# Cached attention decode: V of six head groups loaded through ScalarE's DMA queue beside K on SyncE's queue

## Chip, cores and metric

One core of a Trainium2 chip. The metric is the device time of one execution in microseconds (us). The kernel before takes 203.48 us, median of 3 runs (203.31 to 203.59). The span of a profile is about 1.3 us shorter than the time of the same run.

## The reference

One token goes through a layer norm, a query projection, attention over 4096 cached keys and values in each of 32 heads, an output projection, and a gated MLP. K and V are 33.5 MB each; all weights together are 17 MB, so 84 MB are read for very little arithmetic.

```
q = x_ln @ wq                                # 640 -> 32 heads x 128
scores = einsum("bhqd,bhkd->bhqk", q, k_cache) * 128**-0.5
o = einsum("bhqk,bhkd->bhqd", softmax(scores), v_cache)
h = x + o @ wo
h2 = h + (gelu(h_ln @ w_gate) * (h_ln @ w_up)) @ w_down
```

## The kernel before

The heads are taken in 8 groups of 4. K of a group is one transfer of 4 MB, V another (32 KB of contiguous bytes in each of 128 partitions). The sixteen transfers go in a fixed order through three buffers: transfer n lands in buffer n mod 3 and may be issued when transfer n-3 has been consumed. All are issued by SyncE, so they form one queue.

```
order = [("K", 0), ("V", 0), ("K", 1)]
for G in range(1, NG - 1):
    order += [("K", G + 1), ("V", G)]
order.append(("V", NG - 1))
# K0 V0 K1 K2 V1 K3 V2 K4 V3 K5 V4 K6 V5 K7 V6 V7

def issue(upto):
    while state["next"] < min(upto, len(order)):
        n = state["next"]
        kind, g = order[n]
        # (cut: source, destination)
        landed[n] = [P.dma("sync", dst[...], src[...],
                           consumed[n - NSLOT] if n >= NSLOT else None) for i in range(parts)]
        state["next"] = n + 1
```

K is consumed by four VectorE multiplies (`score_mult`); a chain of identity matmuls on PE (`fold`) and a VectorE reduction sum the products; ScalarE's exponentials of each of the four follow (`score_exp`, which also holds the reduction). V is consumed by 32 matmuls (`pv_group`). PE does them in the order of the list, so V of group G-1 is consumed just after the scores of group G.

```
def scores(G):
    for i in range(4):
        score_mult(4 * G + i)                  # waits for K; the 4th one frees K's buffer
        if i >= 1:
            score_exp(4 * G + i - 1)
    score_exp(4 * G + 3)
    issue(pos[("K", G)] + 1 + NSLOT)           # into K(G)'s buffer: V(G), for G >= 2

for kind, G in order:
    if kind == "K":
        scores(G)
        continue
    # (cut: sums and head sums)
    heads = pv_group(G)                        # frees V's buffer
    issue(pos[("V", G)] + 1 + NSLOT)           # into V(G)'s buffer: K(G+3), for G >= 1
```

After the last V come the loads of the output projection and, into the freed buffers, of the MLP weights.

The softmax here doesn't subtract the row's maximum and nothing guards it: scores larger than these inputs give would overflow.

## Time and profile before

| | before |
|---|---|
| time, median | 203.48 us |
| bytes read | 84.3 MB |
| DMA queue q1 (SyncE), share of 16 engines | 97.8% |
| PE / VectorE / ScalarE busy | 60% / 50% / 30% |
| VectorE waiting for K | 32.9 us, 7 times |

These are lines of the profile's page. The rows `DMA` and `GB/s` cut the span in 40 equal slices: a 9 means that the 16 DMA engines were busy 90% or more of the slice. Below them are the DMA queues with packets, bytes and share of engine time, and the page's list of issues, with median us from issue to landing.

```profile
DMA  9999999999999999999999999999999999999992
GB/s 357 414 417 454 428 415 422 428 451 441 423 422 428 428 444 441 428 417 428 422 448 448 418 422 430 422 441 448 428 425 422 409 428 445 409 405 439 406 412 111
...
q1 hardware_dynamic: 4322, 84.32, 97.8%
...
q10 hardware_dynamic: 2, 0.00, 0.0%
...
slot<-in_A_k_cache_dram SPq DMA_DIRECT2D x8, 4096.0 KB, 21.6
slot<-in_A_v_cache_dram SPq DMA_DIRECT2D x7, 4096.0 KB, 17.7
```

The DMA engines are never without work until the last slice. In the trace's packet records (start, duration, size and queue of every packet, read from the packed trace; no view of the page prints them), successive K and V transfers start 9.7 us apart, a 32 KB packet takes 1.213 us, and 16 engines at that rate move 432 GB/s. 84.3 MB at that rate is 195 us: the kernel runs at its floor but for its start and tail.

Packet times in this text count from the same zero as the profile's timelines. The prediction and the expectations below were written with packet times counted from a zero about 0.35 us later, so their 1.4 or 1.3 us from an issue to its first packet is 1.0 us here, and their 3.8 to 4.5 us is 3.4 to 4.1 us.

The next view gives the busy time of each engine in five stretches: start and end, length, then the engines in the order of its first line (PEld is PE's weight load), the clock granted to PE, the DMA share and GB/s.

```profile
core 0: us, PE busy (x) PEld busy (x) DVE busy (x) ACT busy (x) POOL busy (x), PEclk, DMA share, GB/s
65.00:80.00 15.00, 9.90 (x72) 4.61 (x71) 10.36 (x9) 6.14 (x29) 0.00 (x0) 1.00 0.99 425
80.00:110.00 30.00, 19.17 (x121) 8.43 (x123) 17.49 (x15) 13.10 (x63) 0.00 (x0) 0.83 1.01 433
110.00:120.00 10.00, 5.75 (x35) 2.24 (x25) 5.54 (x4) 0.91 (x3) 0.00 (x0) 0.83 0.99 424
120.00:150.00 30.00, 20.11 (x140) 8.57 (x138) 17.93 (x15) 13.97 (x66) 0.00 (x0) 0.89 1.01 434
150.00:160.00 10.00, 5.55 (x14) 1.97 (x15) 6.41 (x4) 1.17 (x6) 0.00 (x0) 0.66 0.96 415
```

Three lines of VectorE's timeline (start, duration, then the instruction) and one of the table of waits (total us, times, longest) show the rhythm around 58 and 74 us:

```profile
57.65 4.48 DVE L261 TENSOR_TENSOR prod<-slot,qb 128x4096 bf16<-128x4096 bf16 x2
...
66.04 2.28 DVE L261 TENSOR_TENSOR prod<-slot,qb 128x4096 bf16<-128x4096 bf16 x1
...
74.26 4.50 DVE L261 TENSOR_TENSOR prod<-slot,qb 128x4096 bf16<-128x4096 bf16 x2 [3.25 <-DMA slot<-in_A_k_cache_dram]
```
```profile
DVE prod L261 <- DMA slot<-in_A_k_cache_dram: 32.9, 7, 6.7
```

VectorE starts K of group 2 at 57.65 us without waiting, frees its buffer with the fourth multiply at 68.32, and then waits a few us for each later K. While VectorE waits for K, K is on its way, and the DMA engines are busy.

### The profile page before, as it was taken

The page shows a single profiled execution, that of the slowest core. Times are in us where ns is not written, and L with a number is a line of the kernel's source. Part 1 is how long each engine was busy: PE and PEld are TensorE (multiplying, and loading weights), DVE is VectorE, ACT ScalarE, POOL GpSimd, SP SyncE. Part 2 cuts the span into 40 slices and gives each one's busy share as a digit, 9 for nine tenths or more (in the row PEclk, how much of TensorE's full clock was granted, in tenths as well). Part 3 has the DMA queues.
Part 4 walks back from the last instruction along what each step waited for, and adds up shares of the span by engine and source line. Part 5 has one row for each costly group of instructions (what it writes and reads, how often), then busy time and mean ns, then how long its engine had stood idle before and what let it go on. Part 6 is the DMA issues. An engine that isn't in the chain of part 4 may idle for free.

```text
span 202.0 us, 2498 instructions
## 1 busy us (share of the span) xinstructions
PE 121.3 (60%) x1009; PEld 58.5 (29%) x1009; DVE 100.7 (50%) x104; ACT 61.1 (30%) x273; POOL 4.1 (2%) x12
## 2 busy tenths in 40 slices
PE   0108067367749847660978196628744987467395
PEld 0103022112213322230324032312331334267383
DVE  3101179428979739814792677277718760100221
ACT  2011005610563642550156125503640364100101
POOL 7000000000000000000000000000000000000000
PEclk9999859966996999995599979966996699955555
DMA  9999999999999999999999999999999999999992
GB/s 357 414 417 454 428 415 422 428 451 441 423 422 428 428 444 441 428 417 428 422 448 448 418 422 430 422 441 448 428 425 422 409 428 445 409 405 439 406 412 111
DMA packets 4335, 84.47 MB, mean 418 GB/s; under 512 B 482, under 2 KB 868, under 8 KB 1508
## 3 DMA queue, kind: packets, MB, share of 16 engines
q1 hardware_dynamic: 4322, 84.32, 97.8%
q8 instruction: 8, 0.13, 0.3%
q14 instruction: 3, 0.02, 0.0%
q10 hardware_dynamic: 2, 0.00, 0.0%
HBM read 84.31 MB, written 0.00 MB: 417 GB/s over the span
## 4 chain that ended last, share of the span: by engine, by line
DMA 64%; PE 17%; DVE 14%; issue 2%; SPq 2%
DMA slot<-in_A_k_cache_dram 42%; DVE prod L261 12%; PE bank L269 11%; DMA slot<-in_B_w_down_dram 11%; DMA slot<-in_A_v_cache_dram 11%; PE bank L298 3%; SPq L51 2%; DVE sc L276 1%; PE bank L307 1%; PE bank L434 0%; DVE out_row L443 0%; PE bank L318 0%; DVE RT L317 0%
## 5 line engine op out<-in xcount | busy, mean ns | idle before, releaser
L269 PE MATMUL bank<-prod,id_b 128*128 128x512 bf16 x256 | 74.1, 448 | 50.5 <-DVE prod L261 50.5
L261 DVE TENSOR_TENSOR prod<-slot,qb 128x4096 bf16<-128x4096 bf16 x32 | 72.4, 2285 | 32.9 <-DMA slot<-in_A_k_cache_dram 32.9
L280 ACT ACTIVATE p_bd<-sc,zero_t 32x32 bf16<-32x32 f32 x128 | 46.4, 362 | 84.7 <-DVE sc L276 83.5
L269 PEld LDWEIGHTS bank<-prod,id_b 128*128 128x128 bf16 x256 | 26.5, 111 | 98.9 <-DVE prod L261 64.4
L276 DVE TENSOR_REDUCE sc<-bank 128x32 f32<-128x512 f32 x32 | 22.0, 688 | 19.6 <-PE bank L269 19.5
L280 ACT ACTIVATION_READ_ACCUMULATOR p_bd<-sc,zero_t 32x1 f32 x128 | 23.5, 184 | 0.0
L298 PE MATMUL bank<-slot,p_bd 128*16 128x512 bf16 x256 | 18.8, 409 | 3.1 <-ACT p_bd L280 2.5
L298 PEld LDWEIGHTS bank<-slot,p_bd 128*16 128x16 bf16 x256 | 9.7, 93 | 8.3 <-ACT p_bd L280 3.0
L307 PE MATMUL bank<-po_sb,hs 128*16 128x128 f32 x64 | 8.4, 274 | 1.1 <-ACT po_sb L302 1.1
L336 PE MATMUL bank<-aP,arena 128*128 128x1 bf16 x160 | 6.7, 178 | 3.8 <-DMA arena<-in_A_wo_dram 3.8
L404 PE MATMUL bank<-hlnT,slot 128*128 128x1 bf16 (+1 forms) x140 | 6.7, 176 | 3.2 <-DMA slot<-in_B_w_gate_dram 3.2
L302 ACT COPY po_sb<-bank 128x512 f32<-128x512 f32 x8 | 4.7, 585 | 11.1 <-PE bank L298 11.1
L247 PE MATMUL bank<-arena,xlnB 128*32 128x512 bf16 x40 | 4.5, 629 | 5.5 <-DMA arena<-in_A_wq_dram 5.5
L336 PEld LDWEIGHTS bank<-aP,arena 128*128 128x128 bf16 x160 | 6.6, 131 | 3.9 <-DMA arena<-in_A_wo_dram 2.6
L404 PEld LDWEIGHTS bank<-hlnT,slot 128*128 128x128 bf16 (+1 forms) x140 | 6.3, 118 | 4.1 <-issue 3.8
L232 ACT ACTIVATE ln<-ln,eps_t 128x1 f32<-128x1 f32 x2 | 0.6, 294 | 21.6 <-DVE ln L230 21.6
L307 PEld LDWEIGHTS bank<-po_sb,hs 128*16 128x16 f32 x64 | 5.5, 96 | 4.4 <-issue 2.1
L221 PE MATMUL bank<-one_bf,x_row 1*128 1x1 bf16 x5 | 0.4, 177 | 8.2 <-DMA x_row<-in_A_x_dram 8.2
L391 DVE TENSOR_TENSOR hT<-xx,bank 128x5 f32<-128x5 f32 x1 | 0.2, 161 | 10.2 <-PE bank L336 10.2
L251 DVE CAST qb<-bank 128x512 bf16<-128x512 f32 x1 | 0.7, 692 | 8.4 <-PE bank L247 8.4
L247 PEld LDWEIGHTS bank<-arena,xlnB 128*32 128x32 bf16 x40 | 1.6, 139 | 7.6 <-issue 7.6
L322 DVE TENSOR_SCALAR aT<-bank,rz 16x128 bf16<-16x128 f32 x2 | 0.7, 338 | 6.0 <-PE bank L307 6.0
(59 smaller groups left out, 24.7 us busy)
## 6 DMA issues: line engine op xcount, KB each, us to landing
slot<-in_A_k_cache_dram SPq DMA_DIRECT2D x8, 4096.0 KB, 21.6
slot<-in_A_v_cache_dram SPq DMA_DIRECT2D x7, 4096.0 KB, 17.7
arena<-in_A_wq_dram SPq DMA_DIRECT2D x1, 5120.0 KB, 15.0
slot<-in_A_v_cache_dram SPq DMA_DIRECT2D x2, 2048.0 KB, 19.9
arena<-in_A_wo_dram SPq DMA_DIRECT2D x1, 2560.0 KB, 27.5
slot<-in_B_w_gate_dram SPq DMA_DIRECT2D x1, 2160.0 KB, 15.4
arena<-in_A_wo_dram SPq DMA_DIRECT2D x1, 1920.0 KB, 31.6
slot<-in_B_w_up_dram SPq DMA_DIRECT2D x1, 1296.0 KB, 18.1
```

The source lines that it names most:

```text
L51: ev = self.op(eng, lambda e: e.dma_start(out, in_), *deps, dma=True)
L247: i = e.matmul(ps_q[hf][32 * j:32 * j + 32, :], xlnB[:, c, :], wq_j[:, c, j, 4 * hf:4 * hf + 4, :], start=(c == 0), stop=(c == 4))
L251: qa = V(lambda e: e.tensor_copy(qb[:, 0:4, :].rearrange("p g d -> p (g d)"), ps_q[0][:, :]), qd)
L261: m = V(lambda e: e.tensor_tensor(out=prod[:, s % 4, :, :], in0=kt[:, 32 * u:32 * u + 32, :], in1=qb[:, G, :].unsqueeze(1).to_broadcast([1 ...
L269: i = e.matmul(ps_f[s % 2][:, :], id_b[:, :], prod[:, s % 4, :, 16 * b:16 * b + 16], start=(b == 0), stop=(b == 7))
L276: reds[s] = V(lambda e: e.reduce_sum(sc[:, s % 4, :], ps_f[s % 2][:, :].rearrange("p (g d) -> p g d", d=16), axis=AX.X), folds[s], exps.ge ...
L280: x = A(lambda e, j=j: e.activation(p_bd[32 * j:32 * j + 32, G % 2, 32 * (s % 4):32 * (s % 4) + 32, j], sc[32 * j:32 * j + 32, s % 4, :], ...
L298: i = e.matmul(po[a:a + 16, :], p_bd[:, G % 2, 4 * b:4 * b + 4, :].rearrange("p g j -> p (g j)"), vt[:, 4 * b:4 * b + 4, :], start=(b < 4) ...
L302: evs[G] = A(lambda e: e.copy(po_sb[:, G % 2, :], po[:, :]), pvs[G], hds.get(G - 2))
L307: i = e.matmul(ps_a[0:16, 128 * (G // 4):128 * (G // 4) + 128], hs[:, r, 12 - 4 * g:28 - 4 * g], po_sb[:, G % 2, 128 * r:128 * r + 128], s ...
L336: r = e.matmul(ps_p[:, c:c + 1], wo_sb[:, t, i, c::5], aP[:, t, i:i + 1], start=(t == 0 and c == 0 and i == 0), stop=(t == 1 and i == 15), ...
L404: i = e.matmul(ps[0 if m < 13 else 64:128, m:m + 1], ws, hlnT[:, c:c + 1], start=(c == 0 and m == 0), stop=(c == 4), skip_group_check=True)
```

## The change

The intent is to let V travel beside K instead of behind it. V of groups 1 to 6 is issued by ScalarE. The second hunk moves the call of `issue` ahead of the last two groups of exponentials, since ScalarE, which now issues V(G), would otherwise reach the issue only after them. With every load on SyncE that hunk alone would change nothing, because it does not alter the order of any engine's own list (read from the code; not run).

```diff
             w = 128 * DH // parts
-            landed[n] = [P.dma("sync", dst[...], src[...], consumed[n - NSLOT] if n >= NSLOT else None)
+            queue = "scalar" if kind == "V" and 0 < g < NG - 1 else "sync"
+            landed[n] = [P.dma(queue, dst[...], src[...], consumed[n - NSLOT] if n >= NSLOT else None)
                          for i in range(parts)]
@@ def scores(G):
             score_mult(4 * G + i)
+            if i == 3:
+                issue(pos[("K", G)] + 1 + NSLOT)
             if i >= 1:
                 score_exp(4 * G + i - 1)
         score_exp(4 * G + 3)
-        issue(pos[("K", G)] + 1 + NSLOT)
```

(`[...]` marks cut index expressions.)

More of the change, by code (lines that the diff above doesn't have):

```diff
@@ L187, in issue @@
             w = 128 * DH // parts
-            landed[n] = [P.dma("sync", dst[:, i * w:(i + 1) * w], src[:, i * w:(i + 1) * w], consumed[n - NSLOT] if n >= NSLOT else None)
+            queue = "scalar" if kind == "V" and 0 < g < NG - 1 else "sync"
+            landed[n] = [P.dma(queue, dst[:, i * w:(i + 1) * w], src[:, i * w:(i + 1) * w], consumed[n - NSLOT] if n >= NSLOT else None)
                          for i in range(parts)]
```

## The prediction

> **What bounds it now.** The DMA engines. The slice view shows DMA at 9 tenths in 39 of 40 slices; the queue table gives SyncE's queue (q1) 97.8% of the 16 engines' span, 84.3 MB at a mean 417 GB/s. In the trace's packet records the fifteen 4 MB K/V transfers that are not split follow each other every 9.7 us without a gap, and a 32 KB packet takes 1.213 us (27 GB/s an engine, 432 GB/s for 16). All 84.3 MB at that rate is 195 us, so with about 1.4 us of start and 2.5 us of tail some 199 us of the 202 us span is a floor, whichever queue issues. The chain of waits agrees: 64% DMA. VectorE is at 50%; the waits view has it waiting 32.9 us for K (7 times).
>
> **What changes.** No byte, packet or arithmetic instruction is added or removed. Six V loads (25 MB) move to ScalarE's queue. An issue costs 0.33 us on the issuing sequencer (timeline), so ScalarE, idle 84.7 us before its exponentials, pays about 2 us in all, none of it critical. The issue, moved ahead of the last exponentials, waits for the group's last multiply, as they do anyway. SyncE gains nothing by not being held up: transfer n waits for the consumption of n-3, and consumption happens in issue order.
>
> What does change is order. The Trainium skill ("DMA: Bandwidth & Descriptors", section "Issuing engines are not separate DMA queues") says DMAs from both engines run on the same 16 DMA engines and interleave; "Queues, rings and completion order" says round-robin by packet. This trace agrees in one place: the 1.3 KB x load on ScalarE's queue took 1.57 us beside 40 KB packets of 1.51 us. So V(G) will no longer queue behind K(G+1) but halve its rate.
>
> **On the critical path.** My estimate, by replaying the traced durations (9.7 us a transfer alone, 10.1 to 11.8 us from K's landing to the last multiply, 4.7 to 5.7 us from there to the next K issue, 1.4 us from issue to first packet), with equal sharing: K of group 2 lands about 7 us later (54 to 61), VectorE starts it about 4 us later, K of group 4 starts about 4 us later (98), the others 1 to 4 us. But the engines have other work queued then, so lateness costs only where all three buffers are landed and unconsumed. That happens once, near 72 us, for about 1 us; elsewhere the backlog stays positive though thinner. V of the last group then lands about 1 us later (171.6 in the chain), and the 27 us of weights after it follow unchanged.
>
> **Prediction.** 204.5 us, range 202.8 to 208.5. Faster by over 2%: 0.02. Within 2%: 0.76. Slower by over 2%: 0.22.
>
> **What would show it.** Queue table: q1 about 70%, ScalarE's queue (q10) about 29%, sum near 97.5%, same MB. DMA issues: V about 20 us or more to landing (17.7 before), K near 20. A DMA slice below 9 only near 70 to 77 us. VectorE's wait for K up, with alternating long and short waits; ScalarE's busy time the same. The final weights stage as long as before.
>
> **What would make it wrong.** Unequal sharing: if V gets more than half, K is later, and idle DMA time grows to several us per early group. Two streams being slower per byte than one (32 KB packets over 1.22 us at equal load). Slower folds under a 0.5 clock, which empty the thin backlog in several cycles. A faster result would need engines above 27 GB/s, or an idle gap that I overlooked.

## The result

| | before | after |
|---|---|---|
| time, median | 203.53 us (6 runs, 203.31 to 205.04) | 209.28 us (6 runs, 208.87 to 211.11) |
| ratio, 95% interval | | 1.029 (1.024 to 1.034) |
| span of the profile | 202.0 us | 208.1 us |
| bytes read | 84.3 MB | 84.3 MB |
| ScalarE busy | 61.1 us | 61.1 us |

A ratio is the mean time of one kernel's runs over that of the other's runs of the same rounds, so it is not quite the ratio of the medians. The change is slower by 2.9%, above the range of the prediction.

The same lines of the page after. Slices are 5.2 us here; DMA falls below 9 in slices 14 and 15 (67.6 to 78.0 us) and 30 (150.9 to 156.1 us).

```profile
DMA  9999999999999789999999999999979999999992
GB/s 355 394 455 403 447 447 416 409 476 422 405 453 447 321 302 413 460 430 409 447 453 384 384 414 441 441 416 441 428 280 403 409 409 430 426 413 432 409 410 101
...
q1 hardware_dynamic: 3458, 59.15, 66.7%
q10 hardware_dynamic: 866, 25.17, 29.0%
...
slot<-in_A_k_cache_dram SPq DMA_DIRECT2D x8, 4096.0 KB, 23.8
slot<-in_A_v_cache_dram ACTq DMA_DIRECT2D x6, 4096.0 KB, 21.0
slot<-in_A_v_cache_dram SPq DMA_DIRECT2D x1, 4096.0 KB, 33.6
```

The two queues together are at 95.7% of a longer span. The five stretches after:

```profile
65.00:80.00 15.00, 12.55 (x79) 5.43 (x76) 12.28 (x9) 7.15 (x33) 0.00 (x0) 0.93 0.88 359
80.00:110.00 30.00, 15.88 (x80) 5.77 (x80) 14.46 (x12) 8.78 (x41) 0.00 (x0) 0.77 0.99 426
110.00:120.00 10.00, 8.09 (x66) 4.05 (x66) 8.31 (x9) 5.50 (x25) 0.00 (x0) 1.00 0.98 396
120.00:150.00 30.00, 14.35 (x89) 5.66 (x88) 13.81 (x13) 7.83 (x37) 0.00 (x0) 0.77 1.00 433
150.00:160.00 10.00, 7.87 (x63) 3.80 (x62) 8.61 (x7) 6.46 (x31) 0.00 (x0) 1.00 0.84 329
```

The reader should see that the engines move 426 to 433 GB/s where they have work, with two queues as with one, and that the loss sits in three short stretches: 359, 396 and 329 GB/s. To put a number on it, I add the bytes of the packet records in a stretch, divide by 433 GB/s, and call the rest of the stretch lost. This gives 2.6 us lost in 70 to 80 us, 1.0 in 110 to 120 and 2.5 in 150 to 160, against 0.1 in each before. That is about 5.9 us more than before (from unrounded figures), of the 208.1 - 202.0 = 6.1 us by which the spans differ. So nearly the whole loss lies in three places. About 4.0 us of it is time in which engines have no packet (1.9, 0.4 and 1.7 us); most of the rest is slow packets behind each gap: the sixteen that restart the engines at 74 us took 1.7 to 2.1 us each in place of 1.21.

VectorE's timeline shows what precedes the first of them, and ScalarE's and SyncE's queues show the issues (`ACTq`, `SPq`):

```profile
61.64 4.49 DVE L262 TENSOR_TENSOR prod<-slot,qb 128x4096 bf16<-128x4096 bf16 x2 [2.84 <-DMA slot<-in_A_k_cache_dram]
...
70.86 2.28 DVE L262 TENSOR_TENSOR prod<-slot,qb 128x4096 bf16<-128x4096 bf16 x1
...
75.75 4.49 DVE L262 TENSOR_TENSOR prod<-slot,qb 128x4096 bf16<-128x4096 bf16 x2
```
```profile
73.17 0.33 ACTq L51 DMA_DIRECT2D slot<-in_A_v_cache_dram  x1
```
```profile
77.86 0.33 SPq L51 DMA_DIRECT2D slot<-in_A_k_cache_dram  x1
```
```profile
DVE prod L262 <- DMA slot<-in_A_k_cache_dram: 37.8, 5, 12.7
```

K of group 2 is started at 61.64 us, 4.0 us later than before, since it shared the engines with V of group 1 (issued at 43.28). Its last multiply starts at 70.86 and frees the buffer at 73.14; V of group 2 is issued at 73.17. But the packet records show that the data of K of group 3 had all been moved by 73.62 on the slowest engine, and earlier on the others, while V of group 2 has its first packet at 74.15. V of group 1 had also landed (68.02) and was still waiting for its matmuls (75.59). In that moment one buffer is being consumed, two hold landed data, and nothing is left to transfer. The pattern repeats: the last multiplies of groups 4 and 6 come late in the same way, and their V issues (112.87 and 154.30 us) are followed by their first packets 1.0 us later.

### The profile page after: what moved, and what is told of

Its sections match the earlier page's. It is cut to its first block, busy times and chain, and to the rows that moved or that the text cites. A ratio compares the mean times of both kernels' runs of the same rounds, so it can differ in the third digit from the quotient of the medians.

```text
span 208.1 us, 2498 instructions
## 1 busy us (share of the span) xinstructions
PE 116.9 (56%) x1009; PEld 56.2 (27%) x1009; DVE 100.3 (48%) x104; ACT 61.1 (29%) x273; POOL 4.1 (2%) x12
## 3 DMA queue, kind: packets, MB, share of 16 engines
q10 hardware_dynamic: 866, 25.17, 29.0%
## 4 chain that ended last, share of the span: by engine, by line
DMA 66%; PE 14%; DVE 14%; issue 2%; SPq 2%
DMA slot<-in_A_k_cache_dram 46%; DVE prod L262 12%; DMA slot<-in_B_w_down_dram 11%; PE bank L270 10%; DMA slot<-in_A_v_cache_dram 9%; PE bank L299 3%; DVE sc L277 2%; SPq L51 2%; PE bank L308 1%; PE bank L436 0%; DVE out_row L445 0%; PE bank L319 0%; DVE RT L318 0%
## 5 line engine op out<-in xcount | busy, mean ns | idle before, releaser
L270 PE MATMUL bank<-prod,id_b 128*128 128x512 bf16 x256 | 69.9, 426 | 54.4 <-DVE prod L262 54.4
L262 DVE TENSOR_TENSOR prod<-slot,qb 128x4096 bf16<-128x4096 bf16 x32 | 72.4, 2282 | 37.8 <-DMA slot<-in_A_k_cache_dram 37.8
L270 PEld LDWEIGHTS bank<-prod,id_b 128*128 128x128 bf16 x256 | 25.2, 107 | 99.4 <-DVE prod L262 68.0
L299 PE MATMUL bank<-slot,p_bd 128*16 128x512 bf16 x256 | 18.1, 406 | 8.6 <-DMA slot<-in_A_v_cache_dram 6.1
L299 PEld LDWEIGHTS bank<-slot,p_bd 128*16 128x16 bf16 x256 | 8.3, 93 | 15.3 <-DMA slot<-in_A_v_cache_dram 7.3
## 6 DMA issues: line engine op xcount, KB each, us to landing
slot<-in_A_k_cache_dram SPq DMA_DIRECT2D x8, 4096.0 KB, 23.8
```

What stands on the lines that cost most here:

```text
L262: m = V(lambda e: e.tensor_tensor(out=prod[:, s % 4, :, :], in0=kt[:, 32 * u:32 * u + 32, :], in1=qb[:, G, :].unsqueeze(1).to_broadcast([1 ...
L270: i = e.matmul(ps_f[s % 2][:, :], id_b[:, :], prod[:, s % 4, :, 16 * b:16 * b + 16], start=(b == 0), stop=(b == 7))
L299: i = e.matmul(po[a:a + 16, :], p_bd[:, G % 2, 4 * b:4 * b + 4, :].rearrange("p g j -> p (g j)"), vt[:, 4 * b:4 * b + 4, :], start=(b < 4) ...
```

## Experiments

**Theory A.** The loss is one of order. V takes half of the engines from the K that is needed next, K lands late, its buffer comes free late, and by then the other two buffers have landed, so the DMA engines idle. **Rival B.** Issuing from ScalarE costs in itself, by its waits or its late issues. **Rival C.** Two busy queues carry fewer bytes per us than one. All times below are medians, ratios are against the kernel before in the same rounds, and "lost" is the DMA time lost between 44 and 172 us, worked out as above (before 0.7, after 6.5 us). All twelve kernels gave correct results.

### Dose: which V loads go to ScalarE's queue

```diff
-            queue = "scalar" if kind == "V" and 0 < g < NG - 1 else "sync"
+            queue = "scalar" if kind == "V" and g in (1, 3, 5) else "sync"     # odd
+            queue = "scalar" if kind == "V" and g in (2, 4, 6) else "sync"     # even
+            queue = "scalar" if kind == "V" and g == 1 else "sync"             # first
```

(One of the three lines at a time.)

> Only V of groups 1, 3 and 5 on ScalarE's queue, the other three on SyncE's. Theory A: each of these is issued while the next K has most of its 4 MB to go, so K of groups 2, 4, 6 stays late and the three idle gaps stay: 207 to 209.5 us, nearly the whole loss. Rival B or C (a cost per V load on ScalarE's queue, or per byte that two queues carry): half the loss, about 206.4 us.

> Only V of groups 2, 4 and 6 on ScalarE's queue. Theory A: in the order of before these are issued when the K ahead of them has half or less to go, and a queue that joins waits about 3.8 us before its first packet, so they share almost nothing: 203.5 to 204.5 us, no gap. Rival B or C: half the loss, about 206.4 us.

> Only V of group 1 on ScalarE's queue. Theory A: K of group 2 lands at 60 to 61 us in place of 54, one idle gap of about 2 us near 73 us, none later: 205 to 206.5 us. Rival B or C: one sixth of the loss, about 204.5 us.

| | time | ratio (95%) | lost |
|---|---|---|---|
| odd | 211.10 us | 1.039 (1.036 to 1.042) | 7.7 us |
| even | 204.28 us | 1.006 (1.003 to 1.008) | 1.5 us |
| first | 205.56 us | 1.010 (1.009 to 1.012) | 2.6 us |

The stretches of the run with V of group 1 alone on ScalarE's queue:

```profile
65.00:80.00 15.00, 13.34 (x79) 5.69 (x77) 12.12 (x10) 7.15 (x33) 0.00 (x0) 0.87 0.90 366
80.00:110.00 30.00, 17.93 (x96) 7.29 (x93) 18.02 (x15) 12.12 (x58) 0.00 (x0) 0.83 1.01 434
110.00:120.00 10.00, 5.50 (x49) 2.98 (x50) 4.68 (x4) 2.16 (x9) 0.00 (x0) 0.83 0.99 424
```

One moved V load makes one gap (366 GB/s in the first stretch), 30 us after its issue, and none later. Equal numbers of moved loads cost 7.7 us and about 0.9 us, depending on which they are. That refutes a cost per load (B) and a cost per byte on a second queue (C) as the main cause: both expected half the loss in either run. By the packet records the K ahead still has about half of its 4 MB to go (47 to 53%) when an odd V has its first packet; for the even ones it is 5, 25 and 43%. So "share almost nothing" holds for V of group 2 alone: K of groups 5 and 7 were started at 118.08 and 157.99 us in place of 113.12 and 152.10. The first of these delays is followed by the only loss worth naming, 0.8 us near 130 us, so "no gap" was not fully met; the second costs nothing, as the last V and the projection weights had been issued by 150.1 us and kept the engines supplied. In these runs how late a K is does not tell the cost; what else is queued then does. The run "odd" lies above my range of 207 to 209.5 us: its gaps are where they were expected, lost 2.0, 2.0 and 3.4 us, but the third is larger than with all six loads moved. Why, I did not settle.

### One queue, issued by ScalarE

```diff
-            queue = "scalar" if kind == "V" and 0 < g < NG - 1 else "sync"
+            queue = "scalar" if n >= NSLOT else "sync"        # and all weights on "scalar"
```

> Every load from the fourth K/V transfer on, and the weights, issued by ScalarE on its one queue, in the order of the kernel before; SyncE keeps only the first four loads and the output. Theory A (loss comes from K and V sharing the engines through two queues): no sharing, so 203.5 us within 1%, no DMA slice under 9. Rival B (issuing V from ScalarE costs in itself, by the issue or by waits in ScalarE's program): at least as slow as the change, 209 us or more.

Measured: 212.93 us, ratio 1.047 (1.046 to 1.048). This fits rival B at first sight, but the trace shows two faults of the experiment. The fourth transfer, K of group 2, joined on ScalarE's queue while K of group 1 was still moving on SyncE's; K of group 1 was started at 49.36 us in place of 44.18, and a gap of 3.5 us followed in 70 to 80 us. And the output-projection loads stood behind ScalarE's own work and were issued 27 us late, so the engines were nearly empty again from about 174 to 178 us. From 80 to 172 us, on one queue, nothing was lost. I built it again without the handover and with the projection loads issued right behind the last V:

```diff
-    d_x = P.dma("scalar", x_row[:, :], A_x[0, :, :])
-    d_wq = [P.dma("sync", arena[:, :], ...)]
+    d_wq = [P.dma("scalar", arena[:, :], ...)]     # x now on "sync"
@@ issue()
+            queue = "scalar"                        # every load; also wo, w_gate, w_up, w_down
# (cut: the load of ScalarE's activation table, now behind the first K issue)
@@ main loop, after issue() behind pv_group(G)
+        if G == NG - 3:
+            wo_load(...)                            # three calls, moved up from below the loop
```

> Mends the first one-queue test, which shared the engines for one transfer at the handover and issued the output-projection weights 27 us late, both by its own build. Now every load but x, from the first on, is on ScalarE's queue in the order of before, the projection weights right behind the last V. Theory A: 203.5 to 205.5 us (up to 2 us for a later first issue and for ScalarE's own work ahead of the last weights), no DMA gap between 40 and 170 us. Rival B (issuing from ScalarE costs): 209 us or more, or gaps in the middle.

Measured: 203.41 us, ratio 1.000 (0.998 to 1.002). Rival B is refuted: ScalarE can issue every large load and the time is that of the kernel before. The expectation of no gap was not fully met: two of its six runs took 205.3 and 205.5 us, the profile fell on one of these, and it shows 1.6 us lost in 70 to 80 us, with single packets of up to 2.6 us. In that profile K of group 2 was started at 59.09 us and freed its buffer at 70.40, in place of 57.65 and 68.32, and V of group 2 was issued at once, at 70.44. So the late issue follows a late multiply, not other work in ScalarE's list. The other four took 203.4 us. Why the scoring was late in this run I did not look for.

### A fourth buffer

The tile of the query weights is free between the query projection and the output projection. It serves as a fourth buffer for K of groups 2, 4 and 6; transfer n then waits for n-4 (the last V keeps its buffer, and the output-projection weights wait for K of group 6).

```diff
-    view = lambda n: slots[n % NSLOT][...]
+    buf  = lambda n: slots[n] if n < 3 else (slots[0] if n == 15 else (slots + [arena])[n % 4])
+    prev = lambda n: ...            # the last user of that buffer, n - 4 in the steady state
+    view = lambda n: buf(n)[...]
-            landed[n] = [P.dma(queue, ..., consumed[n - NSLOT] if n >= NSLOT else None)
+            landed[n] = [P.dma(queue, ..., consumed[prev(n)] if n >= NSLOT else None)
# (cut: the calls of issue, now up to five transfers ahead, and the wait of the projection weights)
```

> The change with a fourth K/V buffer (the query-weight tile, free between the query projection and the output projection). K and V still share the engines through two queues and K still lands late against its issue, but a landed K can no longer hold the last free buffer. Theory A: no DMA gap, 203.5 to 205 us. Rival C (two busy queues carry fewer bytes per us): 209 us as with the change.

> Control: the kernel before with the same fourth buffer. DMA had no gap to fill, so 203.5 us within 1% under every theory.

| | time | ratio (95%) | lost |
|---|---|---|---|
| change with four buffers | 204.36 us | 1.005 (1.001 to 1.008) | 0.8 us |
| before with four buffers | 203.25 us | 0.999 (0.997 to 1.001) | 0.7 us |

Queues and stretches of the change with four buffers:

```profile
q1 hardware_dynamic: 3458, 59.15, 68.5%
q10 hardware_dynamic: 866, 25.17, 28.8%
```
```profile
65.00:80.00 15.00, 9.70 (x46) 4.02 (x50) 11.47 (x8) 4.96 (x25) 0.00 (x0) 0.79 0.99 424
...
110.00:120.00 10.00, 6.62 (x58) 3.35 (x58) 4.82 (x7) 5.50 (x25) 0.00 (x0) 1.00 1.01 433
...
150.00:160.00 10.00, 6.19 (x56) 3.11 (x54) 3.71 (x4) 5.50 (x25) 0.00 (x0) 1.00 0.98 415
```

The same bytes share the same two queues, and all three gaps are gone. That refutes rival C outright and confirms the part of theory A about the buffers. In the profiled run (204.97 us) the rest lies after 172 us (6.0 us lost there against 4.4), in the stage of the weights; I did not chase it.

### The change without its second hunk

```diff
-            if i == 3:
-                issue(pos[("K", G)] + 1 + NSLOT)
             ...
         score_exp(4 * G + 3)
+        issue(pos[("K", G)] + 1 + NSLOT)
```

> The change without its second hunk: issue is called after the last exponentials again, so ScalarE reaches the V issue about 4.4 us later in each group (last multiply to last exponential). Theory A: the three gaps grow, each by up to 4.4 us: 212 to 221 us. Rival B (cost per issue): the same number of issues, 209 us.

Measured: 213.34 us, ratio 1.049 (1.044 to 1.053); lost 9.0 us, of it 4.9, 2.0 and 1.9 us in the three places. A later issue with the same number of issues costs 4 us more, as theory A has it. The time is near the low end of the range, and not every gap grew: the third shrank from 2.5 to 1.9 us.

### Quarters

Each transfer is cut into four column quarters, one behind the other on its queue, so packets are 8 KB. In the first pair the multiplies of a group wait for all four quarters of K; in the second pair each of the four waits for its own. (The matmuls on V take it quarter by quarter in both pairs.)

```diff
-            parts = 2 if n == len(order) - 1 else 1
+            parts = 4
@@ score_mult
-            landed[n][0], qa, qc, folds.get(s - 4))
+            *landed[n], qa, qc, folds.get(s - 4))     # first pair
+            landed[n][u], qa, qc, folds.get(s - 4))   # second pair
```

> The change with each 4 MB transfer issued as four column quarters one after the other on the same queue, so packets of 8 KB in place of 32; all four awaited before use. If the wait of a queue that joins a busy one (3.8 to 4.5 us against 1.3 us on idle engines) and the late landing of a shared K (1.3 us after its last packet against 0.1 to 0.7) are counted in packets, both shrink: first packet 1.4 to 2.3 us after the issue, landing under 0.6 us after the last packet. V of group 1 then joins earlier (worse for K of group 2), K of groups 4 and 6 too (better), so the time is 206 to 211 us. If they are fixed times, they stay and the time is 209 us.

> Control: the kernel before in 8 KB packets. One queue and no gap: 203.3 to 205 us (an 8 KB packet at the rate of a 32 KB one would take 0.30 us).

> As the first, but each of the four multiplies of a group waits only for its own quarter of K. The last multiply then follows the landing of K by about 3 us in place of 11, so buffers come free about 8 us earlier against K's landing. Theory A (the loss is a free buffer that comes too late): no gap though K and V share as much as before, 203.3 to 205 us. If sharing itself cost time, 207 us or more.

> Control: the kernel before with quarters awaited one by one. VectorE waits less, but DMA has no gap to give back: 203.3 us within 1%.

| | time | ratio to before (95%) | lost |
|---|---|---|---|
| before, all four awaited | 206.93 us | 1.017 (1.016 to 1.019) | 3.5 us |
| change, all four awaited | 211.72 us | 1.041 (1.036 to 1.046) | 9.0 us |
| before, quarter by quarter | 206.98 us | 1.018 (1.016 to 1.019) | 3.5 us |
| change, quarter by quarter | 206.88 us | 1.017 (1.016 to 1.019) | 3.5 us |

All four times missed their expectations at the upper side, mainly for one reason: the kernel in quarters moves its bytes more slowly. Its 8 KB packets took 0.309 us or more, against 0.303 for a quarter of a 32 KB one, and with the small gaps between transfers the steady rate was about 422 GB/s in place of 433. So the pairs must be compared within themselves. All four awaited, the change costs 4.8 us more than its control. Quarter by quarter it costs nothing, although K and V share the engines as much (the packet records show both queues active in most stretches). Here the last multiply follows the landing of K at once, so the buffer is free in time. This isolates the second half of theory A: a late K does harm only through the 10 to 12 us of scoring that still stand between its landing and its buffer's release.

The first pair also measures how long a queue takes to join. With 8 KB packets V of group 1 still had its first packet 3.4 us after its issue (43.78 to 47.21), as with 32 KB ones (43.28 to 46.72). This delay did not shrink with the packet; what it is stays open.

The late landing did shrink, and the packet records show what it is. A transfer ends on each engine with a record of 4 bytes, and it lands 0.3 to 0.6 us after the last of these. In the change, between the last data packet of K of groups 2, 4 and 6 and that record stands one packet of V, of 1.21 us (for group 2: data to 59.93 us, V to 61.14, the 4 bytes at 61.14, landed at 61.61). With 8 KB packets the packet of V between them takes 0.31 us (for group 6: data to 145.05, V to 145.37, landed at 145.89). So the record that ends a transfer takes its turn behind the other queue like a data packet.

No run beat the kernel before: the four-buffer version of it is the same within 0.3%, as a kernel whose DMA engines are never idle has nothing to gain from buffers.

## Why the prediction was wrong

- **The bound: right.** DMA is the bound before and after; 84.3 MB at an unchanged 433 GB/s where there is work.
- **No cost in issuing: right.** ScalarE's busy time is 61.1 us in both, and one queue issued by ScalarE gives ratio 1.000.
- **Interleaving: right.** The queue table shows 25.17 MB on q10, and in 92 to 98 us the packet records give 214 and 220 GB/s to the two queues. V's time to landing rose from 17.7 to 21.0 us.
- **K of group 2: right.** "Lands about 7 us later (54 to 61), VectorE starts it about 4 us later": it landed at 61.61 in place of 54.84, and VectorE started it at 61.64 in place of 57.65.
- **The step that failed** is "That happens once, near 72 us, for about 1 us; elsewhere the backlog stays positive though thinner." It happened three times, for 2.6, 1.0 and 2.5 us. The mechanism was named; terms of the replay were mis-sized. First, it took "1.4 us from issue to first packet" everywhere. That holds on idle engines (1.0 us here), but where the other queue is moving data it is 3.4 to 4.2 us in the change (V of group 1: 43.28 to 46.72; K of group 4: 77.86 to 81.98; K of group 6: 118.58 to 121.97; the last V: 158.98 to 163.17). Second, it names no term for the turn of the 4-byte record: a K that shares the engines to its end lands 1.6 to 1.7 us after its last data packet (groups 2, 4 and 6), against 0.4 to 0.5 us for every K before. K of group 4 was started at 101.17 us, where I had 98 and before had 93.69; these 3.2 us are more than the 1.0 us lost behind it, so by this estimate the second gap would not have opened at the forecast time. I have not redone the replay with the measured terms, so that they account for the third gap as well is not shown.
- **The first gap** was foreseen and came out at 2.6 us in place of "about 1 us". Of this, 1.9 us is idle engines and about 0.7 us the slow first packets, for which the replay had no term. And scoring group 2 took longer: 11.50 us from VectorE's start to the free buffer (61.64 to 73.14) against 10.67 before, with VectorE waiting 1.32 us for the first fold in place of 0.50; the granted clock in these stretches was 0.76 against 0.84. These 0.8 us lie inside the prediction's own range of durations. A backlog that "stays positive though thinner" could not be told from an empty one with durations that it gave as 10.1 to 11.8 and 4.7 to 5.7 us.
- **Two of the missing terms stood in the trace before.** The x load on ScalarE's queue was issued at 1.30 us, beside SyncE's first load, and had its data packet at 6.30, 5.0 us later (in the first us of the program, so other causes can be mixed in). Its data took 0.06 us; its 4-byte record came 1.51 us behind, as long as one 40 KB packet of the other queue. The prediction took the sum, 1.57 us, as a sign of shared data alone.
- **Signs that I named:** the sum of the queues was 95.7%, not "near 97.5%", which alone tells of the gaps. K took 23.8 us to landing, not "near 20". VectorE's wait for K rose to 37.8 us, with 12.7 and 12.5 us before groups 4 and 6 and none before groups 3, 5 and 7: alternating, as said. A DMA slice below 9 was expected only near 70 to 77 us; slice 30 fell too. The weights stage was as long as before: 30.4 us from the last V's landing (171.57) to the end of the span, and 30.9 us after (177.19).
- **The three ways to be wrong** that I listed were unequal sharing, slower bytes and slower folds. The first two are excluded above. The third is seen in the first fold of group 2 alone, the 0.8 us told above: groups 4 and 6 took 11.67 us each from start to free buffer, against 11.83 and 11.67 before. Over the whole run PE's fold matmuls averaged 448 ns before and 426 after, as the page's groups show, an average that hides group 2:

```profile
L269 PE MATMUL bank<-prod,id_b 128*128 128x512 bf16 x256 | 74.1, 448 | 50.5 <-DVE prod L261 50.5
```
```profile
L270 PE MATMUL bank<-prod,id_b 128*128 128x512 bf16 x256 | 69.9, 426 | 54.4 <-DVE prod L262 54.4
```

What stays open: why the gaps differ in size (1.0 us in the middle, 2.5 us around it), why moving only the odd loads costs more than moving all six, what the joining delay is made of, and why single packets behind a gap take up to 2.1 us.

## What to carry to other kernels

When the DMA engines are saturated, as here, a second queue brings no bytes (433 GB/s with one or two); it only changes which transfer lands first, and sharing delays the one that is needed next. With few buffers, ask of each transfer when its buffer comes free, not only when its data come: a late landing plus the time to consume can leave every buffer full and the engines idle. If two streams must share, give them one more buffer or consume in pieces as they land; and when a hand replay leaves margins under the uncertainty of its durations, read it as a risk, not as a "no".

## What the Trainium skill lacked or had wrong

- "DMA: Bandwidth & Descriptors", section "Issuing engines are not separate DMA queues", says that several issuing engines only save the sequencer's issue time. That they bring no bytes holds here (433 GB/s with one queue or two). The page lacks that the interleaving delays the transfer already under way and can cost time: 203.53 to 209.28 us, and even one V load moved cost 1.0%.
- The same page, section "Queues, rings and completion order", describes a round robin by packet. Over a long stretch this agrees (214 and 220 GB/s), but it gives no delay for a queue that joins busy engines: 3.4 to 4.2 us from issue to first packet in the change, against 1.0 us on idle ones, and 3.4 us also with packets of a quarter of the size.
- No page read for this case says how much later a transfer lands beside a second busy queue: 1.6 to 1.7 us after the last data packet of K, against 0.4 to 0.5 us with one queue, because its 4-byte closing record waits for one 32 KB packet of the other queue (1.21 us).
- "DMA: Bandwidth & Descriptors", section "Specifications", gives about 27 GiB/s for an engine; the traces show 32 KB in 1.213 us, which is 27.0 GB/s, or 25.2 GiB/s. Its fabric ceiling of 435 GB/s agrees with the 433 GB/s seen.
